# A delta-rule attention with two expert networks: a third expert's first 128 slots computed early, and another plan for all pieces

## The chip, the cores and the metric

One core of one Trainium2 chip. The metric is the device time of one execution in microseconds (us), the median of several runs. The core has five engines with an instruction stream each: PE (TensorE: matmuls, and weight loads that overlap them), DVE (VectorE), ACT (ScalarE), POOL (GpSimd) and SP (SyncE, which here only starts transfers). An engine executes its stream in order. If its next instruction has to wait, all that stands behind it in that stream waits too.

## The reference

```python
for t in range(768):                  # B=2, H=8, D=48
    y[:, :, t] = einsum(q_t, state)
    v_old = einsum(state, kn_t)
    state = state + beta_t * einsum(kn_t, v_t - v_old)
x = y -> (1536 tokens, 384)
h = x @ w_in                          # 384 -> 2048
P = a0 + a1*h + a2*h^2 + a3*h^3
Q = 1 + |b0|*|h| + |b1|*h^2
x = (P / (Q + 1e-6)) @ w_out          # 2048 -> 384
logits = x @ w_gate                   # 8 experts, argmax
disp[e, slot] = x of the tokens of e  # in token order, up to 384 slots
y = relu(disp @ w1[e]) @ w2[e]        # 384 -> 1024 -> 384
out[token] = prob * y[e, slot]
```

## The kernel before

The work is cut into pieces. Twelve chunks of 64 tokens make the attention; for each group of four chunks a triangular system is solved (`solve`, rounds 0, 1 and 2), with copies of the gram matrix on ACT (lines 247 and 249), turned on DVE (line 256), and results `A` that the next steps take. Two chunks of both batches make a block of 256 tokens, and there are six blocks (0 to 5).

The first network goes by tiles, eight for each block. `s1` computes `h` of a tile (18 matmuls of 256 columns, line 456); `e2` and `e3` compute the rational function with ACT (lines 461 to 483), DVE (465 to 476) and POOL (`zf` 463 and 464, `gl` 484), which leave the two halves `gh` and `gl`; `s2` multiplies them with `w_out` (`acct`, line 498, 12 matmuls a tile; in the last block `acc`, line 516, 18).

When a block is done, its gate runs: logits `lp` on PE (line 550), the choice `oh` on DVE (564), the place of each token among those of its expert (`pp` on PE, 617 to 620, then DVE and POOL), and a table of tokens by slot (`tb` on PE, 638), from which DVE writes the indices `idx` (645). POOL gathers the tokens of an expert by these indices with an indirect transfer. After the gate of block 3 `settle` already writes indices `idx0` (655), by which the first 128 slots of some experts are computed early: `early_x` gathers `ax` (749) and transposes it (`dxp`, 762), `early_h` is the first matrix (`ehp` on PE, 804, 72 matmuls of 128 columns in two halves, then ACT and DVE), `early_y` the second one (`y`, 821, 24 matmuls of 384 columns).

The experts' weights are loaded in eight pieces of 384 KB each (`ws`, line 739), and each is split by ACT (740) and DVE (741) into a high and a low half (`ew`). There is a ring of four staging buffers. All large memory is in six slots that are reused in turn: three of the attention, then that of the first matrix `wi`, then those of the second. The first two experts' weights go where two slots of the attention were, the early tokens (`ax`) into the third. When the last gate's `idx` is written, the rest follows: gathers `xd` (749), `dxp`, `hp` (784, 72 matmuls a group of slots), `hh` on ACT and `hl` on DVE (789, 790), `y`, and a scatter (827). An expert that has had its first 128 slots early has 128 left; the others have 256. The pieces of the other experts' weights are issued after `idx`, between these steps (`fill_`).

The order of all this comes from a table of times, `PLAN`. Each piece is entered with a time, the pieces that it needs, and a function that writes its instructions:

```python
def add(name, time, needs, f):
    todo[name] = (time, needs, f)
...
for name in sorted(todo, key=lambda q: todo[q][0]):
    emit(name)
```

A scheduler behind it then fixes the order on each engine. `EARLY` is the number of experts that begin early, `PLAN["experts"]` the number whose weights are pieces of the table.

Of the kernel before, what the change touches and what calls it, by code (L numbers as in the profile page):

```python
# [20 lines left out]
NCH = S // C  # L21
# [11 lines left out]
XS = 0.125  # L33

BYTOK = range(5)
PLAN = {'tiles': ((94.62, 6.95), (151.99, 6.94), (188.36, 5.73), (232.03, 5.29), (276.15, 3.92), (344.39, 2.58)),
 'lags': (8.77, 6.68, 15.4),
 'u': (50.59, 69.78, 81.54, 98.48, 107.98, 124.54, 157.18, 195.04, 218.05, 237.74, 249.51, 282.48),
 'rel': {'kT': 2.41,
         'loads': 4.55,  # L40
         'values': -10.66,
         'qk': -3.8,
         'lower': -5.93,
         'tk': -2.67,
         's': 10.18,
         'y': 3.45,
         'x': 7.22},
 'norm': (-36.92, 54.42, 110.21),
 'solve': ((-5.44, 3.69), (31.55, 6.74), (156.04, 3.59)),
 'gram': ((-1.03, 1.72), (14.91, 1.55), (123.21, 9.13)),  # L50
 'qk': (10.43, 32.45),
 'conv': (58.22, 0.02),
 'early': (8.43, 7.71),
 'lead': 16.47,
 'gate': (1.01, 2.5),
 'w': (364.51, 1.45),
 'experts': 2,
 'behind': 3,
 'masks': 2,
 'copies': 1,  # L60
 'settle': 310.33,
 'pre': ((362.66, 372.11, 354.38, 372.47), (338.34, 382.38, 397.83, 407.42)),
 'hold': 1}
WN = 4
CA = 2
HB = 3
ZB = 3
GB = 2
EARLY = 2
SETTLE = 3  # L70
ZA = 2
WS = 32.0
# [5 lines left out]
def attention_moe_moe(ctx, tc, kT, qT, k, v, beta, w_io, a, b, w_gate, w1, w2, out, dbg=None):  # L78
# [14 lines left out]
    def slot(shape, dt, name):  # L93
        return slots.tile(shape, dt, tag="slot", name=name)
# [40 lines left out]
    def load_kk(r):  # L135
        kk = st.tile([128, 2, 16, D], F32, tag="raw", name="kk", bufs=2)
        for i in range(2):
            kks[r, i] = kk[:, i]
            nc.sync.dma_start(kks[r, i], k[:, 4 * r + 2 * i:4 * r + 2 * i + 2].rearrange("p c u d -> p (c u) d"))
# [111 lines left out]
    def solve(r):  # L251

        gT = gams.pop(r)
        Wu = Wub[r % 2]
        nc.gpsimd.memset(bufB, 0.0)
        nc.vector.transpose(bufT, Wu.rearrange("p t u -> p (t u)"))
        Lt = bufT.rearrange("p (s t) -> p s t", s=32)
        A = bufA.rearrange("p (s t) -> p s t", s=32)
        nc.vector.scalar_tensor_tensor(A, Lt, -1.0, gT.unsqueeze(1).to_broadcast([128, 32, 32]), ALU.mult, ALU.mult)
        T = bufB.rearrange("p (t s) -> p t s", t=32)  # L260
        nc.vector.tensor_copy(bufB[:, 0:1024:33], gT)
        yield
        for j in range(31):
            m, n = 31 - j, j + 1
            tmp = bufT[:, 0:m * n].rearrange("p (i c) -> p i c", c=n)
            nc.vector.tensor_tensor(  # L266
                tmp, A[:, j, n:32].unsqueeze(2).to_broadcast([128, m, n]), T[:, j:n, 0:n].to_broadcast([128, m, n]), ALU.mult
            )
            nc.vector.tensor_tensor(T[:, n:32, 0:n], T[:, n:32, 0:n], tmp, ALU.add)  # L269
            if j % 4 == 3:  # L270
                yield
        nc.vector.transpose(Wu.rearrange("p t u -> p (t u)"), bufB)  # L272
        ends[r] = nc.vector.transpose(Tt, T.rearrange("p t s -> p s t"))
# [3 lines left out]
    def lower(n, tile_):  # L277
# [6 lines left out]
        for p in range(2):  # L284
            lo, hi = slice(64 * p, 64 * p + 32), slice(64 * p + 32, 64 * p + 64)
            for sl, o in ((lo, 0), (hi, 32)):
                if n < PLAN["copies"]:
                    nc.gpsimd.tensor_copy(Z[sl, :, p, o:o + 32], Wu[sl, :, us].rearrange("p t u -> p u t"))
# [46 lines left out]
    def qk(n, tile_):  # L335
# [6 lines left out]
        for p in range(2):  # L342
            o = slice(64 * p, 64 * p + 64)
            if n < PLAN["masks"]:
                nc.vector.tensor_tensor(G[o, :, p, :], g[o], mask[o].unsqueeze(1).to_broadcast([64, NP, C]), ALU.mult)
# [93 lines left out]
    TILES = []  # L439
# [213 lines left out]
    def settle(tile_):  # L653

        nc.vector.tensor_copy(idx0[:, 0:EARLY], tbl[:, 0:EARLY, 0])
        cn = tile_([128, EARLY], "cn0")
        nc.tensor.matmul(cn, ones16, osum[:, 0:EARLY], start=True, stop=True)
        ad = sm.tile([128, EARLY], F32, tag="mc", name="ad", bufs=1)
        nc.vector.tensor_scalar(ad, cn, -1.0, 128.0, ALU.mult, ALU.add)
        nc.vector.scalar_tensor_tensor(osum[0:1, 0:EARLY], ad[0:1], 0.0, osum[0:1, 0:EARLY], ALU.max, ALU.add)  # L660

# [82 lines left out]
    def gather(e, t0, nt, idx, to=None):  # L744
        res = []
        for t in range(nt):
            xd = to[t] if to else st.tile([128, ROW], F32, tag="t64", name="xd", bufs=3)
            col = idx.shape[-1] // E * e + t0 + t
            nc.gpsimd.indirect_dma_start(
                out=xd[:, :], out_offset=None, in_=rows[:, :], in_offset=bass.IndirectOffsetOnAxis(ap=idx[:, col:col + 1], axis=0),  # L750
            )
            res.append(xd)
        return res

    def expert_x(xds, ps, to=None):
        nt = len(xds)
        xh, xl = to or [el.tile([128, 3, SLOTS], F16, tag=f"x{i}", name="dx") for i in range(2)]
        gg = sm.tile([128, 2], F32, tag="gg", name="gg", bufs=3)
        for t, xd in enumerate(xds):
            xp = ps([128, DM], "dxp")  # L760
            for kt in range(3):
                nc.tensor.transpose(xp[:, 128 * kt:128 * kt + 128], xd[:, 128 * kt:128 * kt + 128], ident)
            cs = slice(128 * t, 128 * t + 128)
            src = xp.rearrange("p (k t) -> p k t", k=3)
            nc.scalar.activation(xh[:, :, cs], src, AF.Copy)
            nc.vector.tensor_tensor(xl[:, :, cs], src, xh[:, :, cs], ALU.subtract)
            nc.vector.tensor_copy(gg[:, t:t + 1], xd[:, DM:ROW])
        return xh, xl, gg
# [82 lines left out]
    def add(name, time, needs, f):  # L851
        todo[name] = (time, needs, f)
# [10 lines left out]
    first = {blk: next(i for i in range(len(TILES)) if TILES[i][0] == blk) for blk in range(len(BLOCKS))}  # L863
    tiles_at, lags = PLAN["tiles"], PLAN["lags"]
    T = [tiles_at[blk][0] + (i - first[blk]) * tiles_at[blk][1] for i, (blk, _) in enumerate(TILES)]
    U = PLAN["u"]
    r0 = PLAN["rel"]
    early = NCH and U[1] + r0["x"]
# [17 lines left out]
    add(("kk", 1), 2.0, [], lambda: load_kk(1))  # L886
    add(("kk", 2), PLAN["norm"][2] - 8, [("norm", 1)], lambda: load_kk(2))
    gens = {r: solve(r) for r in range(3)}
# [31 lines left out]
    for j in range(16):  # L920
        at = PLAN["early"][j] if j < len(PLAN["early"]) else c1 + dc * j
# [20 lines left out]
    def next_weights(e):  # L942
        if e not in wgen:
            wgen[e] = weights(e, got)
        next(wgen[e], None)

    for k_ in range(2 * WN * PLAN["experts"]):
        add(
            ("w", k_), PLAN["w"][0] + PLAN["w"][1] * k_ * 4 / WN, [("w", k_ - 1)] + [(c, n) for n in range(NCH) for c in ("y", "x")],
            lambda k_=k_: next_weights(k_ // (2 * WN))  # L950
        )

    ex, eh = {}, {}
# [3 lines left out]
    def early_x(e):  # L957
        if not ax:
            ax.append(slot([128, 6144], F32, "ax"))
        o = 1024 * EARLY + 1024 * e  # L960
        to = [ax[0][:, o + 512 + 192 * i:o + 704 + 192 * i].bitcast(F16).rearrange("p (k t) -> p k t", k=3) for i in range(2)]
        ex[e] = expert_x(gather(e, 0, 1, idx0, [ax[0][:, o:o + ROW]]), m_tile, to)

    def hold(e, f):
        if e < PLAN["hold"]:
            f()
        else:
            with tc.issue_after(ends["s2"].ins):
                f()

    def early_y(e):
        hh, hl = zip(*(eh[e, i] for i in range(2)))
        expert_y(e, 0, 1, (hh, hl), ex[e], got[e], idx0, lambda: None, m_tile)
# [5 lines left out]
    for e in range(EARLY):  # L979
        at = PLAN["pre"][e]  # L980
        wait = last_s2 if e >= PLAN["hold"] else []
        add(("ex", e), at[0], [("settle",), ("ex", e - 1)] + [("w", 2 * WN * (EARLY - 1))], lambda e=e: early_x(e))
        for i in range(2):
            add(("eh", e, i), at[1 + i], [("ex", e), ("eh", e, i - 1), ("ey", e - 2), ("w", 2 * WN * e + WN - 1)] + [("x", NCH - 1)] + wait,
                lambda e=e, i=i: hold(e, lambda: eh.update({(e, i): early_h(e, ex[e], got[e], i)})))
        add(("ey", e), at[3], [("eh", e, 1), ("w", 2 * WN * e + 2 * WN - 1)] + wait, lambda e=e: hold(e, lambda: early_y(e)))
# [32 lines left out]
    with tc.If(over > SLOTS):  # L1019
# [3 lines left out]
        for e in range(E):  # L1023
            run(weights(e, got2))
            for t0, nt in ((0, 2), (2, 1)):
                x = expert_x(gather(e, t0, nt, idx3), a_tile)
# [61 lines left out]
```

## Time and profile before

| | |
|---|---|
| median of 3 runs | 612.13 us (611.74 to 615.08) |
| the profiled execution | 612.29 us |
| its span, first to last instruction | 610.6 us |
| granted PE clock, mean | 0.909 of full |
| PE, DVE, ACT, POOL busy | 511.2, 464.3, 401.0, 289.7 us |
| moved by DMA | 59.33 MB |

The rows further down are from this one execution. A clock of 1.00 is 2.4 GHz and 0.50 is 1.2 GHz. Busy times overlap between engines. A row of a timeline may stand for several equal instructions in a row (x12), and its duration is then from the first one's start to the last one's end, with some 0.16 us of pipeline at the end of a matmul.

### The profile page before, as it was taken

What the parts mean: (1) busy time and instruction counts of PE and PEld (TensorE: products, weight loads), DVE (VectorE), ACT (ScalarE), POOL (GpSimd) and SP (SyncE); (2) the same over time, 40 slices, a digit from 0 to 9 for tenths busy, and PEclk for the clock granted to TensorE, in tenths of its full rate; (3) what the DMA queues carried; (4) which work ended last, traced back from release to release, by engine and by line L of the source; (5) the groups of instructions that cost most, each with busy time, mean ns of one, the idle gap of its engine ahead of it and who ended that gap; (6) DMA issues with size and microseconds to landing.
All of it is one profiled execution on the core that took longest, in us unless ns stands there. A gap on an engine that the chain in (4) does not pass through costs nothing.

```text
span 610.6 us, 14736 instructions
## 1 busy us (share of the span) xinstructions
PE 511.2 (84%) x5952; PEld 425.5 (70%) x5952; DVE 464.3 (76%) x868; ACT 401.0 (66%) x778; POOL 289.7 (47%) x282
## 2 busy tenths in 40 slices
PE   5415785888888998996999999989995998799993
PEld 5415674676667887885888888788884886567761
DVE  4899998999985999997657377999735777873320
ACT  6754667787889965858779779967641666661110
POOL 7402115877773765844546565668543222212111
PEclk9955557897989998999899999979998899999998
DMA  8911313555441010010020103370105788861001
GB/s 240 269 39 54 91 41 117 157 149 171 146 145 28 1 40 27 4 40 1 1 54 2 28 28 104 106 233 27 28 12 163 207 264 283 252 225 42 17 16 32
DMA packets 42159, 59.33 MB, mean 97 GB/s; under 512 B 25550, under 2 KB 29172, under 8 KB 42082
## 3 DMA queue, kind: packets, MB, share of 16 engines
q1 hardware_dynamic: 40034, 52.78, 28.9%
q0 software_dynamic: 2048, 5.52, 3.1%
q8 instruction: 49, 0.80, 0.6%
q14 instruction: 28, 0.23, 0.1%
HBM read 52.76 MB, written 6.30 MB: 97 GB/s over the span
## 4 chain that ended last, share of the span: by engine, by line
PE 37%; DVE 31%; DMA 12%; ACT 10%; issue 5%; POOL 2%; SPq 0%; POOLq 0%; DVEq 0%; ACTq 0%
PE h L456 8%; PE acct L498 7%; DMA ws<-in_w_dram 6%; PE y L821 6%; DVE A L266 6%; DVE A L269 5%; PE hp L784 4%; DMA raw<-in_w_io_dram 3%; ACT A L290 2%; DVE h L475 2%; DVE pf L465 2%; DVE ew L741 2%; PE acc L516 2%; DVE pf L474 2%; DVE pf L466 2%
## 5 line engine op out<-in xcount | busy, mean ns | idle before, releaser
L456 PE MATMUL h<-x,wi 128*128 128x256 f16 x864 | 117.1, 284 | 16.5 <-DVE wi L201 5.5
L456 PEld LDWEIGHTS <-wi 128*128 128x128 f16 x864 | 81.0, 101 | 36.8 <-issue 10.0
L484 POOL TENSOR_TENSOR gl<-pf,gh 128x512 fp32r<-128x512 f32 x48 | 65.5, 1365 | 47.5 <-ACT gh L483 42.0
L741 DVE SCALAR_TENSOR_TENSOR ew<-ws,ew 128x768 f16<-128x768 f32 x64 | 62.9, 997 | 17.3 <-ACT ew L740 16.9
L740 ACT ACTIVATE ew<-ws 128x768 f16<-128x768 f32 x64 | 52.9, 841 | 23.3 <-DMA ws<-in_w_dram 22.7
L784 PE MATMUL hp<-dx,ew 128*128 128x256 f16 (+1 forms) x576 | 59.8, 265 | 9.1 <-DVE hl L790 8.3
L463 POOL TENSOR_SCALAR zf<-za,cf 128x512 f32<-128x512 f32 x48 | 42.1, 876 | 52.6 <-ACT za L461 52.2
L464 POOL TENSOR_TENSOR zf<-zf,za 128x512 f32<-128x512 f32 x48 | 65.0, 1353 | 3.7
L784 PEld LDWEIGHTS <-ew 128*128 128x128 f16 x576 | 52.5, 101 | 16.1 <-issue 10.1
L827 POOL DMA_INDIRECT out_dram<-yo,idx x16 | 18.5, 1158 | 84.5 <-DVE yo L825 70.2
L821 PE MATMUL y<-ew,hh 128*128 128x384 f16 x224 | 55.9, 326 | 0.0
L474 DVE SCALAR_TENSOR_TENSOR pf<-pf,cf,h 128x512 f32<-128x512 f32 x48 | 35.5, 739 | 17.2 <-ACT h L473 16.9
L465 DVE TENSOR_TENSOR pf<-pf,h 128x512 f32<-128x512 f32 x48 | 32.4, 676 | 16.1 <-ACT pf L462 12.8
L498 PE MATMUL acct<-wo_h,gh 128*128 128x384 f32 x160 | 42.2, 379 | 1.7 <-ACT gh L483 1.6
L266 DVE TENSOR_TENSOR A<-A,A 128x31 f32<-128x31 f32 (+15 forms) x93 | 41.2, 443 | 2.3
L269 DVE TENSOR_TENSOR A<-A,A 128x31 f32<-128x31 f32 (+15 forms) x93 | 41.0, 440 | 2.4
L472 ACT ACTIVATE za<-zf,qc 128x512 f32<-128x512 f32 x48 | 34.6, 721 | 11.7 <-POOL zf L464 11.4
L498 PE MATMUL acct<-wo_h,gl 128*128 128x384 f32 x160 | 39.1, 356 | 2.1 <-POOL gl L484 2.1
L323 POOL TENSOR_TENSOR A<-v,nrm 64x384 f32<-64x384 f32 x24 | 23.2, 967 | 35.8 <-PE S L373 26.3
L290 ACT ACTIVATE A<-A 32x256 f32<-32x256 f32 x44 | 28.7, 651 | 16.3 <-DVE A L272 13.1
L789 ACT ACTIVATE hh<-hp 128x512 f16<-128x512 f32 (+1 forms) x32 | 16.9, 536 | 32.9 <-PE hp L784 32.9
L462 ACT ACTIVATE pf<-h,cf 128x512 f32<-128x512 f32 x48 | 37.2, 775 | 1.0 <-POOL gl L484 0.9
(188 smaller groups left out, 1271.3 us busy)
## 6 DMA issues: line engine op xcount, KB each, us to landing
ws<-in_w_dram SPq DMA_DIRECT2D x64, 384.0 KB, 4.1
raw<-in_w_io_dram SPq DMA_DIRECT2D x16, 768.0 KB, 4.6
rows<-xr SPq DMA_DIRECT2D x12, 192.5 KB, 2.9
kk<-in_k_dram SPq DMA_DIRECT2D x6, 384.0 KB, 4.6
A<-in_k_dram SPq DMA_DIRECT2D x24, 96.0 KB, 2.8
v<-in_v_dram SPq DMA_DIRECT2D x12, 192.0 KB, 3.2
A<-in_qT_dram SPq DMA_DIRECT2D x24, 96.0 KB, 2.8
A<-in_kT_dram SPq DMA_DIRECT2D x10, 192.0 KB, 3.6
```

What stands on the lines that cost most here:

```text
L266: nc.vector.tensor_tensor(tmp, A[:, j, n:32].unsqueeze(2).to_broadcast([128, m, n]), T[:, j:n, 0:n].to_broadcast([128, m, n]), ALU.mult)
L269: nc.vector.tensor_tensor(T[:, n:32, 0:n], T[:, n:32, 0:n], tmp, ALU.add)
L456: s1_last[i] = nc.tensor.matmul(h[:, w * m:w * m + w], ww[:, kt, js], x[:, kt, 0:w], start=(n == 0), stop=(n == 8))
L464: nc.gpsimd.tensor_tensor(zf, zf, za, ALU.mult)
L465: nc.vector.tensor_tensor(pf, pf, h, ALU.mult)
L474: nc.vector.scalar_tensor_tensor(pf, pf, cf[:, 0:1], h, ALU.add, ALU.mult)
L484: nc.gpsimd.tensor_tensor(gl, pf, gh.bitcast(F32), ALU.subtract)
L498: ends["s2"] = nc.tensor.matmul(acc[blk][t], g[:, o:o + 128], ww[:, j, :], start=(j == 0 and m == 0), stop=(j == 15 and m == 2))
L740: nc.scalar.activation(ws[:, 2 * m, cs], s, AF.Copy, scale=MS)
L741: nc.vector.scalar_tensor_tensor(ws[:, 2 * m + 1, cs], s, MS, ws[:, 2 * m, cs], ALU.mult, ALU.subtract)
L784: nc.tensor.matmul(hp[:, g, 0:ns], w[:, kt, 128 * (f + g):128 * (f + g) + 128], xx[:, kt, 0:ns], start=(n == 0), stop=(n == 8))
L821: nc.tensor.matmul(y, hx[f // 4][:, f % 4, cs], w[:, f, :], start=(n == 0), stop=(n == 23))
```

## The change

Three experts instead of two have their first 128 slots computed early, and the weights of the third go as pieces of the table into the slot of `wi`. That slot is free when the last `s1` has been done, so its eight pieces wait for that and for the first early gather. All numbers of the plan are new. The diff without the larger part of the plan's numbers:

```diff
-PLAN = {'tiles': ((94.62, 6.95), (151.99, 6.94), ...
+PLAN = {'tiles': ((87.39, 6.96), (135.34, 7.24), ...
...
- 'experts': 2,
+ 'experts': 3,
+ 'w2': (378.99, -0.47),
  'behind': 3,
  'masks': 2,
- 'copies': 1,
- 'settle': 310.33,
- 'pre': ((362.66, 372.11, 354.38, 372.47), (338.34, 382.38, 397.83, 407.42)),
- 'hold': 1}
+ 'copies': 3,
+ 'settle': 272.89,
+ 'pre': ((322.1, 322.01, 316.46, 336.37), (277.99, 342.7, 356.3, 363.26), (333.47, 349.5, 364.59, 405.2)),
+ 'hold': 4}
...
-EARLY = 2
+EARLY = 3
+
+FIRST = 2
...
     for k_ in range(2 * WN * PLAN["experts"]):
         add(
-            ("w", k_), PLAN["w"][0] + PLAN["w"][1] * k_ * 4 / WN, [("w", k_ - 1)] + [(c, n) for n in range(NCH) for c in ("y", "x")],
+            ("w", k_), PLAN["w"][0] + PLAN["w"][1] * k_ * 4 / WN if k_ < 2 * WN * FIRST else PLAN["w2"][0] + PLAN["w2"][1] * (k_ - 2 * WN * FIRST),
+            [("w", k_ - 1)] + [(c, n) for n in range(NCH) for c in ("y", "x")] + [("s1", len(TILES) - 1), ("ex", 0)] * (k_ >= 2 * WN * FIRST),
             lambda k_=k_: next_weights(k_ // (2 * WN))
         )
...
-        add(("ex", e), at[0], [("settle",), ("ex", e - 1)] + [("w", 2 * WN * (EARLY - 1))], lambda e=e: early_x(e))
+        add(("ex", e), at[0], [("settle",), ("ex", e - 1)] + [("w", 2 * WN * (FIRST - 1))], lambda e=e: early_x(e))
```

What moves is seen in the order of the instructions. In the changed kernel the lines have numbers that are higher by 3 (by 4 after line 949).

On PE, at the end, between the last gate's place matmuls (`pp`, line 618) and the first `dxp` of gathered rows, the order before is this; of each run of equal matmuls the first is shown (12 `ehp`, 12 `y`, `tb`, 12 `y`):

```order
L618 MATMUL pp<-oh,low_136 128x16
L620 MATMUL pp<-oh,ones_138 128x8
...
L804 MATMUL ehp<-ax,ew 128x128
...
L821 MATMUL y<-ew,ax 128x384
...
L638 MATMUL tb<-v_5759,pm 128x8
...
L821 MATMUL y<-ew,ax 128x384
...
L762 MATMUL dxp<-ident,xd 128x128 x3
```

In the changed kernel the same place reads as follows (6 `ehp`, 12 `y`, 11 `ehp`, `y`, `ehp`, `tb`, 11 `y`, 24 `ehp`, 13 `y`, and 11 `y` behind the first three `dxp`):

```order
L621 MATMUL pp<-oh,low_136 128x16
...
L807 MATMUL ehp<-ax,ew 128x128
...
L641 MATMUL tb<-v_5765,pm 128x8
...
L824 MATMUL y<-ew,ax 128x384
...
L807 MATMUL ehp<-ax,ew 128x128
...
L824 MATMUL y<-ew,ax 128x384
...
L765 MATMUL dxp<-ident,xd 128x128 x3
...
L824 MATMUL y<-ew,ax 128x384
```

Between the last `acc` and `tb` there were 72 `ehp` and 12 `y`; now there are 120 and 13. Behind `tb` there are 24 `ehp` that were not there.

On PE, in the gate of block 3, between the logits `lp` and the place matmul `pp` that takes `oh`, there were 18 `h` and 12 `acct` matmuls, and steps of the last chunk (`Y`, `xp`):

```order
L550 MATMUL lp<-wg,xT 128x8 x6
...
L456 MATMUL h<-x_3589,wi 128x256
...
L498 MATMUL acct<-wo_h,gh 128x384 x4
...
L400 MATMUL xp<-ident,ys 128x128
L403 MATMUL xp<-ident,ys 64x64 x2
...
L618 MATMUL pp<-oh,low_136 128x16
```

Now 46 `h` of later tiles and 26 `acct` stand there:

```order
L553 MATMUL lp<-wg,xT 128x8 x3
...
L459 MATMUL h<-x_3631,wi 128x256
...
L501 MATMUL acct<-wo_h,gh 128x384 x4
...
L459 MATMUL h<-x_4442,wi 128x256
...
L501 MATMUL acct<-wo_h,gl 128x384 x4
...
L459 MATMUL h<-x_4441,wi 128x256
...
L621 MATMUL pp<-oh,low_136 128x16
```

More of the first network's work has moved in between, and the chunk's steps have moved out.

On ACT, in solve round 2, the copies of the gram (lines 247 and 249) stood in a row behind an `h` (line 473); the rows show that `h`, the first of six such rows of three copies, and what follows the fourth:

```order
L473 ACTIVATE h<-za 128x512
L247 ACTIVATE A_87<-gram 32x8x32 x2
L249 ACTIVATE A_87<-gram 32x256
...
L483 ACTIVATE gh<-pf 128x512
L472 ACTIVATE za<-zf,qc 128x512
```

Now two of these rows of three stand ahead of the `h` of the same tile (line 476 of the changed kernel):

```order
L250 ACTIVATE A_87<-gram 32x8x32 x2
L252 ACTIVATE A_87<-gram 32x256
...
L464 ACTIVATE za<-h 128x512
L465 ACTIVATE pf<-h,cf 128x512
L476 ACTIVATE h<-za 128x512
L410 ACTIVATE x_1878<-xp 128x3x64
```

Six copies have moved ahead of it, and twelve are left behind it.

## Rows read from the trace of the kernel before

**Rows 1.** The page's first part: engine, busy us, share of the span, instructions.

```profile
PE 511.2 (84%) x5952; PEld 425.5 (70%) x5952; DVE 464.3 (76%) x868; ACT 401.0 (66%) x778; POOL 289.7 (47%) x282
```

**Rows 2.** Windows; stretch, length, busy us of PE, PEld, DVE, ACT, POOL, PEclk, DMA.

```profile
200.00:283.00 83.00, 78.79 (x855) 67.73 (x852) 82.35 (x163) 58.71 (x116) 54.18 (x52) 0.98 0.09 21
...
473.00:550.00 77.00, 67.76 (x589) 54.16 (x590) 60.52 (x94) 49.58 (x77) 18.05 (x16) 0.96 0.79 245
```

**Rows 3.** PE's waits (whole span, then 270 to 460): us, times, longest.

```profile
PE hp L784 <- DVE hl L790: 8.3, 3, 4.0
...
PE e L300 <- ACT A L304: 3.6, 1, 3.6
PE pp L618 <- DVE oh L564: 2.7, 1, 2.7
...
PE dxp L762 <- DMA ax<-rows,idx: 0.9, 2, 0.8
```

**Rows 4.** Windows behind three waits of PE; columns as in rows 2.

```profile
288.10:294.90 6.80, 6.80 (x81) 5.46 (x77) 3.26 (x5) 4.85 (x9) 4.53 (x5) 0.50 0.00 0
...
398.50:404.10 5.60, 5.60 (x19) 5.60 (x19) 5.60 (x12) 3.17 (x6) 4.45 (x5) 0.50 0.62 181
...
473.00:479.20 6.20, 5.50 (x42) 4.94 (x43) 3.94 (x9) 3.56 (x6) 1.94 (x2) 0.50 0.57 188
```

**Rows 5.** PE's timeline at the end: start, us, line, operation, [idle before <-releaser].

```profile
437.92 4.13 PE L804 MATMUL ehp<-ax,ew 128*128 128x128 f16 x71
...
453.77 0.38 PE L516 MATMUL acc<-gl,wo_h 128*128 128x256 f32 x1 [0.85 <-POOL gl L484]
...
455.66 0.28 PE L516 MATMUL acc<-gh,wo_l 128*128 128x256 f32 x1
...
463.93 0.24 PE L638 MATMUL tb<-v,pm 128*128 128x8 f16 x4
464.03 2.11 PE L821 MATMUL y<-ew,ax 128*128 128x384 f16 x12
472.99 0.87 PE L762 MATMUL dxp<-ident,xd 128*128 128x128 f32 x3 [6.85 <-DMA xd<-rows,idx]
...
560.40 8.02 PE L784 MATMUL hp<-dx,ew 128*128 128x256 f16 x72
```

**Rows 6.** PE's timeline: two of three `hp` that waited for `hl`.

```profile
511.57 2.13 PE L784 MATMUL hp<-dx,ew 128*128 128x256 f16 x18 [2.70 <-DVE hl L790]
...
532.42 2.12 PE L784 MATMUL hp<-dx,ew 128*128 128x256 f16 x18 [4.01 <-DVE hl L790]
```

**Rows 7.** DVE's timeline: `idx`, and the weight pieces 24 and 33 to 34.

```profile
464.21 0.17 DVE L645 TENSOR_TENSOR idx<-tbl,tb 128x16 uint32<-128x16 f32 x1 [0.40 <-PE tb L638]
...
508.90 0.96 DVE L741 SCALAR_TENSOR_TENSOR ew<-ws,ew 128x768 f16<-128x768 f32 x1 [0.91 <-ACT ew L740]
...
523.18 1.94 DVE L741 SCALAR_TENSOR_TENSOR ew<-ws,ew 128x768 f16<-128x768 f32 x2
```

**Rows 8.** ACT's and DVE's timeline in solve round 2.

```profile
186.87 1.24 ACT L247 ACTIVATE A<-gram 32x256 f32<-32x256 f32 x2
...
188.58 0.74 DVE L466 SCALAR_TENSOR_TENSOR pf<-pf,cf,h 128x512 f32<-128x512 f32 x1
...
196.65 1.25 DVE L256 STREAM_TRANSPOSE A<-A 128x1024 f32<-128x1024 f32 x1 [6.73 <-ACT A L247]
```

**Rows 9.** Timelines of PE, DVE and POOL: indices and gathers, early and last.

```profile
409.09 0.24 PE L638 MATMUL tb<-v,pm 128*128 128x8 f16 x4
...
410.73 0.15 DVE L655 CAST idx<-tbl 128x2 uint32<-128x2 f32 x1
...
429.08 1.17 POOL L749 DMA_INDIRECT ax<-rows,idx  x1 [1.88 <-issue]
...
433.74 0.52 PE L762 MATMUL dxp<-ident,ax 128*128 128x128 f32 x3 [0.76 <-DMA ax<-rows,idx]
...
465.68 1.32 POOL L749 DMA_INDIRECT xd<-rows,idx  x1 [4.86 <-DVE ew L741]
```

More of the change, by code (lines that the diff above doesn't have):

```diff
@@ L35 @@
 BYTOK = range(5)
[L36 to L39, printed above, removed]
+PLAN = {'tiles': ((87.39, 6.96), (135.34, 7.24), (173.58, 5.61), (228.86, 5.43), (261.99, 3.31), (304.16, 2.45)),
+ 'lags': (7.85, 6.14, 15.25),
+ 'u': (50.56, 68.24, 74.12, 91.1, 101.22, 117.16, 149.8, 190.86, 211.68, 233.44, 248.05, 258.63),
+ 'rel': {'kT': 1.1,
          'loads': 4.55,
-         'values': -10.66,
+         'values': -10.08,
          'qk': -3.8,
-         'lower': -5.93,
+         'lower': -6.09,
          'tk': -2.67,
-         's': 10.18,
+         's': 4.15,
          'y': 3.45,
[L47 to L56, printed above, removed]
- 'experts': 2,
+         'x': 9.91},
+ 'norm': (-25.56, 44.75, 94.01),
+ 'solve': ((-22.39, 0.64), (42.7, 7.45), (165.7, 2.86)),
+ 'gram': ((-14.02, 7.74), (23.31, 1.73), (115.83, 7.46)),
+ 'qk': (5.57, 34.64),
+ 'conv': (31.48, 1.38),
+ 'early': (5.78, 5.58),
+ 'lead': 13.0,
+ 'gate': (0.7, 3.03),
+ 'w': (291.4, 7.94),
+ 'experts': 3,
+ 'w2': (378.99, -0.47),
  'behind': 3,
  'masks': 2,
- 'copies': 1,
- 'settle': 310.33,
- 'pre': ((362.66, 372.11, 354.38, 372.47), (338.34, 382.38, 397.83, 407.42)),
- 'hold': 1}
+ 'copies': 3,
+ 'settle': 272.89,
+ 'pre': ((322.1, 322.01, 316.46, 336.37), (277.99, 342.7, 356.3, 363.26), (333.47, 349.5, 364.59, 405.2)),
+ 'hold': 4}
 WN = 4
```

## The prediction

> **What bounds the kernel now.** The page's table of engines came first: TensorE (PE) is busy 511.2 of 610.6 us [rows 1], so what can be won is PE's idle time, PE's work at the low clock, and work that PE need not do. The busy time by stage came next. Between 200 and 283 us PE is busy 78.79 of 83 us and VectorE (DVE) 82.35: DVE is full there, and PE goes at its pace. From 473 to 550 us (the experts behind the last gate) PE is busy 67.76 of 77 and DVE 60.52 [rows 2]. The lists of waits tell which idle time has a cause the change touches: 8.3 us in three waits of an expert's `hp` for `hl`, and between 270 and 460 us 3.6 us for `A` (solve round 2), 2.7 us for `oh` (gate of block 3) and 0.9 us for the early gathers [rows 3]. The windows behind such gaps show a second price. After the waits of 3.6, 2.7 and 6.85 us the granted clock reads 0.50, the 1.2 GHz level instead of 2.4, for 6 to 7 us with PE nearly all the time busy [rows 4]: 5.6 us of work there would be 2.8 at the full clock, so such a spell costs about 3 us beside the wait. The wait of 0.85 us for `gl` [rows 5] was followed by none.
>
> The chain at the end, in PE's timeline [rows 5]: the last `acc` matmul of the first expert network starts at 455.66, `tb` of the last gate at 463.93, DVE writes `idx` at 464.21 [rows 7], and the first `dxp` of gathered rows starts at 472.99, after a gap of 6.85 us. From there on PE works and waits to its end near 600.3, 136.1 us behind `idx`, and the kernel ends with it. What stands ahead of `tb` delays everything behind it; what stands between `tb` and `dxp` is free as far as the gap reaches; what stands behind is paid in full.
>
> **The end, term by term**, against the profiled 612.29 us (0.16 over the median).
>
> (1) Ahead of `tb`, PE now has 120 `ehp` matmuls instead of 72 behind the last `acc`, and 13 `y` instead of 12. 71 `ehp` took 4.13 us, 0.16 of it the end of the pipeline: 0.056 us each. 12 `y` took 2.11 and in the same way 1.95, 0.1625 each [rows 5]. 48 x 0.056 + 0.16 = **+2.85**.
>
> (2) Between `tb` and `dxp` stand 24 `ehp` and 24 `y` instead of 12 `y`: 5.24 us instead of 1.95. The gathers leave as long after `idx` as before, so the gap shrinks from 6.85 to about 3.6 and the end doesn't move: **0**. I keep the low clock behind it, since 2.7 and 3.6 were followed by it; without it about -3.
>
> (3) Behind the gather, the third expert has one tile of 128 slots left instead of two. A full expert's 72 `hp` of 256 columns take 8.02 us with the pipeline's end, 7.86 without [rows 5]; a 128-column expert takes 72 x 0.056 = 4.03. `hp`: 6 x 7.86 + 2 x 4.03 = 55.2 before, 5 x 7.86 + 3 x 4.03 = 51.4 after. `y`: 14 tiles of 24, 3.9 us each, against 13, of which 11 matmuls moved behind the first `dxp` (1.8): 54.6 and 52.5. `dxp`: one tile of three transposes less, 0.33. In all **-6.3**.
>
> (4) The `hl` waits: 2.70, 4.01 and 1.64 us (the first two in [rows 6]). `hl` stands on DVE behind weight pieces. Before, it came behind 25, 38 and 48 pieces in experts 3, 4 and 5. The changed kernel has 40 pieces in place of 48 left, since the third expert's eight land earlier, and has 24 and 33 ahead of `hl` of experts 3 and 4. The pieces come at the pace of their transfers: the 24th ended 45.6 us behind `idx`, the 33rd 59.9 behind (the first of a pair in its row) [rows 7], and an `hl` takes 0.6 more. At expert 3, PE stood there 44.7 us behind `idx` (511.57 - 2.70 - 464.21); the third expert's shorter `hp` (7.86 - 4.03), the transposes and (5) take 4.7 off and the 11 `y` and some waiting of its narrow groups put up to 2.9 on: 42.9, a wait of 3.3 us to 46.2. At expert 4 it stands some 12.5 us later (18 `hp` 2.0, transposes 0.7, one tile of `y` 3.9, 54 `hp` 5.9): 58.7 against 60.5, 1.8 us. At expert 5 nothing is left to wait for. 5.1 for 8.35, **-3.25**. Bounds: all 8.35 gone, or a wait as long as before.
>
> (5) The 11 `y` behind the first `dxp` cover the wait for `dx` there, 0.58 us: **-0.6**.
>
> The end: **-7.3** (+2.85 - 6.3 - 3.25 - 0.6). Bounds -12 (no low clock, less waiting for pieces) and 0 (the waits for `hl` grow by what (3) saves).
>
> **Ahead of the end.** (6) Solve round 2. ACT (ScalarE) makes 18 copies of the gram from 186.87 on, nearly in a row, and DVE idles 6.73 us for them until 196.65 [rows 8]. The `h` (natural exponential) ahead of all 18 has 6 of them ahead of it in the changed order and 12 behind, 3.3 us less after the tile work that DVE waits with, so that about half of the wait goes. Seven tile operations of DVE, 0.66 us each (0.74 with the part that overlaps the next [rows 8]), that stood between the start and the end of the solve stand behind it: 4.6 us. But PE comes to the step that needs the solve's result after 1.2 tiles of `h` and one of `acct` less, 22 x 0.11 + 12 x 0.16 = 4.3 us by the 256 and 384 columns of [rows 5], so the earlier result first makes up for a shorter cover. I take **-3** (0 when the cover is what binds, -9 when the 3.6 us wait of [rows 3] goes with its spell too and the rest).
>
> (7) Gate of block 3. PE waits 2.7 us for `oh` [rows 3] and then runs at the low clock [rows 4]. Behind `lp` stood 18 `h` and 12 `acct`, now 46 and 26: by the 0.11 us of 256 columns and the 0.1625 of 384 [rows 5] 3.9 and 9.3 us, less some 2 of the chunk's steps that have gone, so that 3.4 us more cover 2.7. 2.7 + 2.8 would be 5.5; **-4**, because DVE is full there and `oh` itself may come later. Bounds -6 and 0.
>
> (8) The early gathers. `tb` of gate 3 started at 409.09 and `idx0` at 410.73, done some 1.8 us later than the former, from `idx` to the gather 1.5 us (464.21 to 465.68 at the last gate), and from the gather's start to the second `dxp` 4.7 us (429.08 to 433.74) [rows 7, 9]. That is 8 us; before, 20 us of other work lay between `tb` and the gather. In the changed order PE has from that `tb` to the first `dxp` 18 `h`, 4 `acct`, 19 `acc` and a few small ones, 5.2 us at these prices. **+3** less 0.8 of the wait that it replaces, so **+2.2**; +5.2 when the low clock follows.
>
> (9) The last tile's `gl`: 72 `ehp` of expert 0 (4 us) now stand between the `acc` groups and could cover the wait of 0.85 [rows 5], but weight pieces now stand on ACT and DVE in front of this tile's `gh`. I leave the wait as it is and count the third expert's `dxp`: **+0.4**.
>
> Sum ahead of the end: -3 - 4 + 2.2 + 0.4 = **-4.4**. Altogether -11.7: **600.6 us**.
>
> **One price that could be wrong.** The split of an expert's pass of 256 columns into two of 128 rests on 0.056 us for a 128-column matmul with its weight load [rows 5]. The Trainium skill, "TensorE: Matmul & The Clock Gate", section "Back-to-back issue gap", gives about 81 ns for a stream of weight load and matmul at 128 columns, and says that 56 ns holds for an isolated one alone. By it 144 matmuls would cost an estimated 11.7 us in place of 8.1. This trace disagrees: 71 in a row took 0.056 us each. Were the price of a 128-column stream 0.025 us higher, term (1) would be +1.2, and terms (2) and (3) by 48 more matmuls some 1.8 worse: 603.6 us.
>
> **Rivals.**
> A. *The tail alone pays*: terms (6) to (9) cancel, because DVE is full up to 283 us [rows 2] and what PE saves at one place it waits for at the next. 612.29 - 7.3 = 605.0.
> B. *The last tile is late*. The third expert's pieces now stand on DVE ahead of the last tile's last polynomial step (two of them) and on ACT ahead of its `gh` (two more). If these land at the pace of the tail's pieces, 1.9 us (45.6 us over 24, [rows 7]), `gl` comes 4.3 us later, 3.5 of it beyond the cover, with a spell of 3 behind: 600.6 + 6.5 = 607.1, near the edge of no change.
> C. *Slower*: between 200 and 283 us. DVE is full there, and the changed order puts the steps of ten tiles 3.5 to 7 us of DVE work later. PE, with 4.2 us idle [rows 2], would run dry: 7 us of waits and three spells of 3 give +16, 616.6. It ends slower by over 0.5% from 14.8 us of new idle time and spells on; for it speaks that every gap near 3 us there has its spell, against it that DVE's total at the milestones of each block stays within a few us.
> D. *The change doesn't do what it says*: the third expert's weights, which wait for the last `h` matmul and the first early gather, aren't there for the 72 `ehp` ahead of `tb`. Eight pieces at 1.9 us each are 15 us; between the last `h` and that place lie 18 to 20 us of PE's work [rows 5]. A miss of 5 us there would give 605.6.
> E. *By the price above*: 603.6.
>
> **How the numbers follow.** The forecast as summed has 0.48, A 0.20, B 0.10, C 0.12, D 0.05, E 0.03, better than 595 us 0.02. The forecast's own range is 595 to 606 (terms (4), (6) and (7) between their bounds). A change of 0.5%, 3.06 us, is about what the three runs (611.74 to 615.08) can tell from none: faster is below 609.23 and slower above 615.35. Faster: 0.48 + 0.20 + half of B + D, E and the better case, 0.83, of which I take 0.07 off for terms that I may have missed: 0.76. Slower: C nearly whole, 0.11. Same: 0.13. The range leaves out C and the far end: 592 to 612.
>
> **What would show it.** (1) `tb` of the last gate some 2.85 us later behind the last `acc`. (2) A gap of about 3.6 us before `dxp`, clock 0.50 behind it. (3) and (4): PE's end some 126 us behind `idx` in place of 136, and two waits for `hl`. (6) The wait of DVE for the gram copies halved. (7) No wait for `oh` and no 0.50 near 400 us. (8) A wait of 2 to 3 us for `ax`. Wrong would be: PE less than 78 us busy in the 83 us up to 283 (C), a wait of `acc` for `gl` of over 2 us (B), or a wait of `ehp` for `ew` (D).

## The result, and the profile after

The changed kernel takes 606.75 us (median of 4 runs, 604.26 to 607.29) against 613.36 for the kernel before (4 runs beside it, 611.74 to 615.08): a ratio of 0.9884, 95% interval 0.9841 to 0.9927. It is 1.2% faster. Ratios, here and below, are of fast executions alone and so need not be the quotient of two medians, which are of all of them. The profiled execution took 604.26 us (the shortest of its four), 8.03 less than the one of before, and that difference splits at one place, the last `acc` matmul.

The changed kernel's timeline of PE (start, us, line, operation, idle before it and its releaser) answers to [rows 5]:

```profile
444.97 4.18 PE L807 MATMUL ehp<-ax,ew 128*128 128x128 f16 x72
...
452.75 4.06 PE L824 MATMUL y<-ew,ax 128*128 128x384 f16 x24 [0.96 <-DVE ax L812]
...
458.68 0.28 PE L519 MATMUL acc<-gh,wo_l 128*128 128x256 f32 x1
...
469.79 0.24 PE L641 MATMUL tb<-v,pm 128*128 128x8 f16 x4
...
471.68 1.50 PE L807 MATMUL ehp<-ax,ew 128*128 128x128 f16 x24
...
476.81 0.52 PE L765 MATMUL dxp<-ident,xd 128*128 128x128 f32 x3 [1.52 <-DMA xd<-rows,idx]
```

The last `acc` starts at 458.68 where it was 455.66, 3.02 us later. PE's last matmul (PE's end, below) starts at 592.21 where it was 600.18, so the stretch behind `acc` is 10.99 us shorter.

Within that stretch: `acc` to `tb` is 11.11 us where it was 8.27 (+2.84). `idx` to the first `dxp` is 6.74 where it was 8.78 (-2.04). From there to PE's end it is 115.40 where it was 127.19 (-11.79). DVE's and POOL's timelines of the changed kernel, and SP's, show why the second is shorter; they answer to [rows 7, 9]:

```profile
470.07 0.17 DVE L648 TENSOR_TENSOR idx<-tbl,tb 128x16 uint32<-128x16 f32 x1 [1.51 <-PE tb L641]
470.71 1.28 POOL L752 DMA_INDIRECT xd<-rows,idx  x1 [4.18 <-DVE idx L648]
471.14 2.94 SPq L742 DMA_DIRECT2D ws<-in_w_dram  x4
```

The first gather now starts 0.64 us behind `idx`, ahead of the four weight pieces. Before, it started 1.47 behind `idx` [rows 9].

The waits for `hl`, in PE's timeline (they answer to [rows 6], 8.35 us before):

```profile
501.99 1.17 PE L787 MATMUL hp<-dx,ew 128*128 128x128 f16 x18 [0.96 <-DVE hl L793]
...
506.64 4.09 PE L787 MATMUL hp<-dx,ew 128*128 128x256 f16 x36 [0.71 <-DVE hl L793]
...
525.70 2.12 PE L787 MATMUL hp<-dx,ew 128*128 128x256 f16 x18 [2.86 <-DVE hl L793]
```

They sum to 4.53 us. The windows of the changed kernel (columns as in [rows 2]):

```profile
200.00:283.00 83.00, 75.77 (x836) 65.46 (x836) 82.21 (x157) 55.91 (x112) 51.12 (x49) 0.98 0.09 20
...
456.00:473.00 17.00, 17.00 (x217) 15.12 (x215) 10.67 (x33) 6.69 (x13) 3.90 (x7) 1.00 0.32 101
473.00:550.00 77.00, 69.22 (x647) 54.24 (x645) 56.07 (x92) 43.97 (x72) 21.17 (x20) 1.00 0.71 231
```

Two things are to be seen: the clock behind the last gap is 1.00 (the spell at 0.50 of [rows 4] is gone in this execution), and PE is 3 us less busy between 200 and 283 us than before, while DVE is as full.

At the gate of block 3, `pp` has no wait any more, but two others stand in front of it, and the clock is at half behind them (PE's timeline, and a window):

```profile
386.82 1.01 PE L388 MATMUL Y<-A,A 112*64 112x48 f32 x16 [1.22 <-ACT A L365]
388.84 0.47 PE L403 MATMUL xp<-ident,ys 128*128 128x128 f32 x1 [1.00 <-ACT ys L390]
...
409.88 0.17 PE L621 MATMUL pp<-oh,low 128*128 128x16 f16 x1
```

```profile
388.80:395.00 6.20, 6.16 (x33) 4.58 (x34) 6.20 (x8) 6.03 (x11) 3.40 (x3) 0.53 0.40 121
```

### The profile page after: what moved, and what is told of

It is laid out like the page before. It is cut to its first block, busy times and chain, and to the rows that moved or that the text cites. A ratio compares the mean times of both kernels' runs of the same rounds, so it can differ in the third digit from the quotient of the medians.

```text
span 602.5 us, 14884 instructions
## 1 busy us (share of the span) xinstructions
PE 503.4 (84%) x6024; PEld 421.3 (70%) x6024; DVE 472.2 (78%) x870; ACT 393.4 (65%) x772; POOL 293.0 (49%) x290
## 4 chain that ended last, share of the span: by engine, by line
DVE 38%; PE 30%; ACT 12%; issue 8%; DMA 7%; POOL 4%; SPq 0%; DVEq 0%; POOLq 0%; ACTq 0%
PE y L824 7%; DVE A L272 7%; DVE A L269 7%; PE h L459 6%; DMA ws<-in_w_dram 4%; PE hp L787 4%; DVE ew L744 4%; PE acct L501 4%; ACT A L250 3%; DVE h L478 2%; DVE pf L468 2%; DVE pf L469 2%; DVE pf L479 2%; DVE pf L477 2%; POOL zf L467 1%
## 5 line engine op out<-in xcount | busy, mean ns | idle before, releaser
L459 PE MATMUL h<-x,wi 128*128 128x256 f16 x864 | 115.0, 284 | 9.0 <-ACT x L410 3.8
L744 DVE SCALAR_TENSOR_TENSOR ew<-ws,ew 128x768 f16<-128x768 f32 x64 | 68.4, 1089 | 11.5 <-ACT ew L743 11.2
L466 POOL TENSOR_SCALAR zf<-za,cf 128x512 f32<-128x512 f32 x48 | 44.2, 922 | 65.0 <-ACT za L464 64.3
L787 PE MATMUL hp<-dx,ew 128*128 128x256 f16 (+1 forms) x576 | 53.8, 252 | 6.1 <-DVE hl L793 4.5
L787 PEld LDWEIGHTS <-ew 128*128 128x128 f16 x576 | 47.8, 98 | 11.6 <-issue 6.9
L824 PE MATMUL y<-ew,hh 128*128 128x384 f16 x208 | 51.7, 326 | 0.0
L272 DVE TENSOR_TENSOR A<-A,A 128x31 f32<-128x31 f32 (+15 forms) x93 | 44.6, 479 | 2.4
L269 DVE TENSOR_TENSOR A<-A,A 128x31 f32<-128x31 f32 (+15 forms) x93 | 44.2, 476 | 2.5
L501 PE MATMUL acct<-wo_h,gh 128*128 128x384 f32 x160 | 40.8, 370 | 1.7 <-ACT gh L486 1.7
L501 PE MATMUL acct<-wo_l,gh 128*128 128x384 f32 x160 | 38.6, 356 | 0.0
L476 ACT ACTIVATE h<-za 128x512 f32<-128x512 f32 x48 | 28.6, 596 | 12.0 <-DVE pf L469 8.4
```

Source lines behind the costliest of these rows:

```text
L269: nc.vector.tensor_tensor(tmp, A[:, j, n:32].unsqueeze(2).to_broadcast([128, m, n]), T[:, j:n, 0:n].to_broadcast([128, m, n]), ALU.mult)
L459: s1_last[i] = nc.tensor.matmul(h[:, w * m:w * m + w], ww[:, kt, js], x[:, kt, 0:w], start=(n == 0), stop=(n == 8))
L501: ends["s2"] = nc.tensor.matmul(acc[blk][t], g[:, o:o + 128], ww[:, j, :], start=(j == 0 and m == 0), stop=(j == 15 and m == 2))
L744: nc.vector.scalar_tensor_tensor(ws[:, 2 * m + 1, cs], s, MS, ws[:, 2 * m, cs], ALU.mult, ALU.subtract)
L787: nc.tensor.matmul(hp[:, g, 0:ns], w[:, kt, 128 * (f + g):128 * (f + g) + 128], xx[:, kt, 0:ns], start=(n == 0), stop=(n == 8))
L824: nc.tensor.matmul(y, hx[f // 4][:, f % 4, cs], w[:, f, :], start=(n == 0), stop=(n == 23))
```

## Experiments

Eight kernels. Ratios are against the kernel before on the same chip, with their 95% intervals.

**Each half of the change alone.** The new plan with two early experts:

```diff
- 'experts': 3,
+ 'experts': 2,
...
-EARLY = 3
+EARLY = 2
```

> The new plan with two early experts, as before. Theory: the new plan by itself puts the last acc about 3 us later and pays nothing at the end, 614 to 617 us. Rival: the new plan carries the gain by itself, 605 to 609 us.

Measured: 615.16 us, ratio 0.9991 (0.9959 to 1.0023). Its last `acc` starts at 456.57, 0.91 us later than before and not 3; `idx` to PE's end is 136.21 us (135.97 before). So the theory had the time right, and the plan alone neither pays nor costs more than the 2.5 us that the interval leaves open.

The old plan with a third early expert:

```diff
- 'experts': 2,
+ 'experts': 3,
+ 'w2': (420.0, -0.47),
...
- 'pre': ((362.66, 372.11, 354.38, 372.47), (338.34, 382.38, 397.83, 407.42)),
+ 'pre': ((362.66, 372.11, 354.38, 372.47), (338.34, 382.38, 397.83, 407.42), (374.5, 390.5, 405.6, 446.2)),
...
-EARLY = 2
+EARLY = 3
...
```

> The old plan with a third early expert added (its pieces and steps at the new plan's distance behind the last tile). Theory: the third expert alone takes 11 us off the end (2.8 later at tb, 13.8 less from idx to the end) and nothing is lost ahead of it: 601 to 604 us. Rival: it gains only with the new plan, because here its pieces or its steps come too late: 609 to 614 us.

Measured: 614.45 us, ratio 0.9986 (0.9949 to 1.0023). The theory had the end right in sign and not in size, and was wrong about what lies ahead; the rival's claim, that it gains only with the new plan, held. `acc` to `tb` is 11.49 and `idx` to PE's end 125.79, so that in all the stretch behind the last `acc` is 6.96 us shorter. But that `acc` starts at 466.77, 11.11 us later than before. ACT's and PE's timeline of this run show where part of it went:

```profile
459.06 0.84 ACT L743 ACTIVATE ew<-ws 128x768 f16<-128x768 f32 x1 [1.51 <-DMA ws<-in_w_dram]
459.81 0.47 ACT L768 ACTIVATE ax<-dxp 128x384 f16<-128x384 f32 x1
460.23 0.84 ACT L743 ACTIVATE ew<-ws 128x768 f16<-128x768 f32 x1
460.98 0.61 ACT L486 ACTIVATE gh<-pf 128x512 fp32r<-128x512 f32 x1
...
461.65 0.50 PE L519 MATMUL acc<-gh,wo_h 128*128 128x256 f32 x2 [3.20 <-ACT gh L486]
...
463.40 0.58 PE L519 MATMUL acc<-gl,wo_h 128*128 128x256 f32 x1 [1.25 <-POOL gl L487]
```

The last tile's `gh` stands on ACT behind pieces of the third expert that wait for their transfers, and PE waits 4.45 us for it and for `gl`. This is rival B, in the old plan. In the changed kernel `gh` comes behind such pieces too, but PE has the 72 `ehp` and 24 `y` of expert 0 to do meanwhile. Of the 11.11 us, 3.01 were there before the order differs on DVE, ACT or POOL (the same `pp` at 401.50 where it was 398.49, last section). Of the other 8.10, 3.60 are these waits (0.85 before); the rest was not taken apart, but the granted clock is 0.83 from 433 to 443 us and 0.60 from 461.2 to 467.

Put together, the four kernels say more than each half. In the new plan too the third expert can be seen by itself, because the plan alone and the changed kernel have the same order on DVE, ACT and POOL up to 443 us. Counted from the `pp` of block 3's gate (407.62 and 409.88) the last `acc` starts 48.95 us later with two early experts and 48.80 with three: nothing is lost. In the old plan it is 57.17 and 65.27. From `idx` to PE's end the third expert takes 14.07 us off in the new plan and 10.18 in the old one. So what the plan is worth is that it takes up the third expert's work ahead of the end, where the old plan pays 8.10 us for it.

**The cover.** The old plan with three experts again, with expert 0's early matmuls moved behind the last tile's `h`:

```diff
- 'pre': ((362.66, 372.11, 354.38, 372.47), ...
+ 'pre': ((362.66, 373.5, 376.0, 378.0), ...
```

> The old plan with a third early expert (the run that gained nothing), with expert 0's 72 early matmuls moved from ahead of the last tile's h to between its acc groups, as in the changed kernel. Theory: the third expert's pieces hold up gh of the last tile by some 5 us on ACT and DVE, and the changed kernel pays nothing for it only because PE has these 72 matmuls to do meanwhile; with the cover the acc waits of 3.2 and 1.25 us and the low clock behind them go, 606 to 610 us. Rival: what the old plan with three experts loses is lost earlier: 612 to 615 us.

Measured: 611.32 us, ratio 0.9955 (0.9926 to 0.9983). The waits of `acc` for the last tile are down to 0.67 us, as the theory had it, but the time lies between theory and rival: a wait of 2.28 us of `y` for `ax` comes in its place, and the clock in the windows from 430 to 450 us is 0.81 and 0.85 behind the waits for the early gathers. From the common `pp` (399.79) to the last `acc` it is 64.92 us, against 65.27 in the run before it, so in the profile the cover won almost nothing; the ratio is lower than that run's 0.9986, but the two intervals overlap. The reverse, the changed kernel with those matmuls moved ahead of the last tiles' `h`:

```diff
- 'pre': ((322.1, 322.01, 316.46, 336.37), ...
+ 'pre': ((322.1, 300, 300, 336.37), ...
```

> The changed kernel with expert 0's 72 early matmuls moved ahead of the last tiles' h, so that they no longer stand between the last tile's acc groups. Theory: PE then waits 3 to 5 us for gh and gl of the last tile, with a spell of low clock behind: 610 to 614 us. Rival: the cover isn't needed, 605 to 608 us.

Measured: 614.86 us, ratio 0.9986 (0.9947 to 1.0024), a little over the theory's range, so the whole gain is gone. PE's, DVE's and POOL's timelines, and a window of it:

```profile
451.34 0.27 PE L641 MATMUL tb<-v,pm 128*128 128x8 f16 x4 [3.20 <-DVE pm L634]
...
447.87 3.42 DVE L634 TENSOR_TENSOR pm<-ps,io 128x512 f16<-128x512 f32 x1
...
448.24 2.49 POOL L487 TENSOR_TENSOR gl<-pf,gh 128x512 fp32r<-128x512 f32 x2
...
463.88 1.04 POOL L830 DMA_INDIRECT out_dram<-yo,idx  x1 [13.16 <-DVE yo L828]
464.93 1.29 POOL L487 TENSOR_TENSOR gl<-pf,gh 128x512 fp32r<-128x512 f32 x1
...
466.27 0.38 PE L519 MATMUL acc<-gl,wo_h 128*128 128x256 f32 x1 [3.09 <-POOL gl L487]
```

```profile
450.00:460.00 10.00, 8.66 (x44) 5.67 (x45) 9.77 (x14) 3.51 (x5) 0.72 (x1) 0.66 0.64 188
```

The wait for `gl` has the expected size but another cause. ACT's `gh` ends at 460.83, and POOL begins `gl` only at 464.93, because the scatter of expert 0's rows stands ahead of it and waits for `yo`. The wait of `tb` for `pm`, with the low clock behind it, was not expected. The 72 matmuls had not covered it: in the changed kernel they stand behind this `tb` (444.86, then `ehp` from 444.97). There `pm` took 0.68 us on DVE and here 3.42, with two `gl` on POOL at the same time. The last `acc` starts at 468.58, 9.9 us later than in the changed kernel, while `idx` to PE's end is 122.65 us, as there (122.14). So the place of these matmuls is worth the whole gain, but this run does not show that they are worth it as a cover for `gh`: by moving them it changed what waits for what on POOL and DVE too.

**What stands ahead of `tb`.** The kernel before with work added there and nothing else:

```diff
+        if last:
+            dm = a_tile([128, DM], "dm")
+            for i in range(18):
+                nc.tensor.matmul(dm, pm[:, 0, 0:128], got[0][2][:, 0, :], start=(i == 0), stop=(i == 17))
         tb = tile_([128, 2, E], "tb")
```

> The kernel before with 18 matmuls of 384 columns added ahead of the last tb, into a tile that nothing reads (2.9 us of PE work, as much as the change adds there; nothing of the result changes). Prediction's step: all of it delays the end, idx to the first dxp stays at 8.8 us and idx to the end at 136. Theory: in the kernel before it is not idx that releases the last gather but the transfer of the block's rows, which lands 1 us behind idx, by when four weight pieces stand ahead of the gather; with tb 2.9 us later the gather starts 0.4 to 0.6 us behind idx and ahead of them, idx to dxp is 6 to 7 us, and the end comes about 1 us later instead of 2.9.

Measured: 615.14 us, ratio 1.0022 (0.9991 to 1.0054). `acc` to `tb` is 11.20 us, 2.93 more, and from the end of `acc` to PE's end 143.86 where it was 144.24: in the profile nothing of the 2.93 arrives. (2.63 come back at the gather, below, and 0.68 behind `dxp`. The medians, 615.14 and 614.54, differ by 0.6; the interval reaches up to 3.3 us, so the times alone decide nothing here.) PE's and POOL's timeline, and a window:

```profile
468.55 0.24 PE L642 MATMUL tb<-v,pm 128*128 128x8 f16 x4
469.27 1.48 POOL L753 DMA_INDIRECT xd<-rows,idx  x1 [6.75 <-DVE idx L649]
...
474.98 0.90 PE L766 MATMUL dxp<-ident,xd 128*128 128x128 f32 x3 [4.22 <-DMA xd<-rows,idx]
```

```profile
474.00:480.00 6.00, 3.62 (x24) 3.05 (x25) 2.38 (x6) 2.44 (x4) 2.96 (x3) 0.50 0.93 312
```

`idx` (468.83) to `dxp` is 6.15 us where it was 8.78: the gather starts 0.44 us behind `idx`. In the kernel before it started 1.47 behind. The second transfer of the last block's rows, which the gather reads, was issued there about 462.9 and such a one took 2.3, so it landed about 465.2; the gather followed at 465.68, and the four weight pieces had started at 465.27. The same split runs through all ten kernels: in four (this one, the changed kernel, no cover, and the changed kernel with copies 1) the gather starts 0.44 to 0.64 us behind `idx`, and `idx` to `dxp` is 5.92 to 6.74 us; in the six others it starts 1.14 to 2.04 behind, and `idx` to `dxp` is 8.22 to 8.99. In those six the profile names an `ew` step of DVE as the releaser, but the first of these starts 0.08 or 0.09 us behind `idx` in all ten, and the weight pieces start 1.06 or 1.07 behind it in all ten. What differs is the rows' transfer: in the four SP has issued it 2.4 to 4.2 us ahead of `idx`, in the six only 1.3 to 2.0, and there the gather starts 2.7 to 3.3 us behind that issue. The gap of 4.22 us still has the low clock behind it.

**The low clock behind the gap.** The kernel before with 40 matmuls added between `tb` and `dxp`:

```diff
+    with tc.issue_after(ends["idx"].ins):
+        dm = a_tile([128, DM], "dm")
+        for i in range(40):
+            nc.tensor.matmul(dm, got[0][2][:, 0, 0:128], got[0][2][:, 0, :], start=(i == 0), stop=(i == 39))
```

> The kernel before with 40 matmuls of 384 columns added between the last tb and the first dxp of gathered rows, into a tile that nothing reads (6.5 us of PE work in the gap of 6.85; nothing of the result changes). Theory: the gap costs a second time by the low clock behind it, so that with PE busy the granted clock stays at 1.00 behind dxp and the time is about 3 us shorter, 611 against 614, idx to the end 133 us for 136. Rival: the clock falls all the same or nothing behind dxp gains by it, because hl and the weight pieces set the pace there: no change or 1 to 2 us more.

Measured: 618.42 us, ratio 1.0025 (0.9988 to 1.0062). This doesn't decide whether the spell costs anything: the scheduler put nine transposes `dxp` in a row behind the added work in place of three and then `hp`, and PE's timeline has new waits there, with the low clock behind them:

```profile
476.38 1.02 PE L762 MATMUL dxp<-ident,xd 128*128 128x128 f32 x6 [1.74 <-DMA xd<-rows,idx]
...
480.55 5.60 PE L784 MATMUL hp<-dx,ew 128*128 128x128 f16 x51 [2.97 <-DVE dx L766]
```

The gap itself was closed (0.24 us), and the gathers behind the first set the pace instead.

**The copies on POOL.** One number of the new plan taken back, and the same number put into the old plan:

```diff
- 'copies': 3,
+ 'copies': 1,
```

> The changed kernel with one of three POOL copies per solve round taken back (copies 1 as before, all else of the new plan). Theory: the copies on POOL slow DVE's solve steps that run at the same time (lines 269 and 272 of the changed kernel took 88.8 us in the first 283 us where before they took 82.0) and DVE is full there, so the last acc comes 3 to 4 us earlier and the time is 602 to 604 us. Rival: the order of tiles and chunks in the new plan costs it, not the copies: 605 to 608 us, solve steps slower or not.

```diff
- 'copies': 1,
+ 'copies': 3,
```

> The kernel before with copies 3 and nothing else. Theory: the solve steps take 5 to 7 us more of DVE and the time is 615 to 617 us. Rival: the copies cost nothing, since ACT is relieved as much as DVE is slowed: 611 to 614 us.

Measured: 617.12 us (ratio 1.0034, 1.0007 to 1.0061) and 626.61 us (1.0190, 1.0140 to 1.0239). The first is 10 us slower than the changed kernel and the second 10 us over its theory; neither theory nor rival held in either. DVE's 186 solve steps take 82.0 us before, 88.8 in the changed kernel, 81.3 with copies back at 1; but put into the old plan copies 3 makes 83.5 of 82.0. The theory's cause is wrong for most of this. The number counts chunks: with 3, chunks 0 to 2 have their four copies each on POOL, between 51 and 68 us in the changed kernel, and no later chunk has any. Of the 6.8 us that the changed kernel's steps take more, 4.8 lie in solve round 2 (200 to 281 us), where POOL makes no copies and runs `zf` and `gl`. The times say nothing of the copies either: each number re-deals thousands of rows of the order on PE, and the run with copies 1 waits 4.47 us for the last tile's `gl`. Neither run measures the copies by themselves.

## Why the prediction came out as it did

The sign and the range held (600.6 forecast, 606.75 measured, 592 to 612). The two halves of the sum did not: the end gave -10.99 for -7.3, and what lies ahead of it +3.02 for -4.4. That their sum came within 6 us is in part luck, since one half missed by 3.7 and the other by 7.4 the other way.

The step that failed is "Sum ahead of the end: -3 - 4 + 2.2 + 0.4 = -4.4". The plan alone moves the last `acc` by +0.9 us and the time not at all, and 2.26 of the 3.02 were there at the same `pp` of two equal orders (409.88 and 407.62), so they are no work of the third expert. Rival A (terms (6) to (9) cancel) is the nearest, at 605.0 for 606.75 measured, but it kept the end at -7.3, so its number is in part luck too. Waits alone, (6) to (9) gave -1.3, -0.5, +0.8 and +0.1. Term by term:

- (6) DVE's wait for the gram copies fell from 6.73 to 2.6 us, somewhat more than forecast, and PE's wait of 3.6 became one of 2.3 at about the same place, with a shorter spell behind it (granted clock 0.74 over the next 6.5 us). That the earlier copies for the most part made up for the shorter cover is read from these rows and was not tested.
- (7) The wait for `oh` went, as forecast; two waits of 1.22 and 1.00 us some 20 us earlier took its place, with a clock of 0.53 behind them. I had priced the removed wait with its spell, as if the spell belonged to the wait. It does not: behind these two waits the clock was 1.00 in the plan alone, and behind the wait for `oh` it was 1.00 in two of five kernels (last section). My own trace had waits of 2.70 and 4.01 us [rows 6] with 1.00 behind them.
- (8) The waits for the early gathers are 0.81 us for `ax` and 0.94 for `gg`, 1.75 for 0.9 before: +0.8, not +2.2.
- (9) The wait of `acc` for `gl` went, and one of `y` for `ax` (0.96) came.

The sign that I had set for C was there (PE 75.77 us busy between 200 and 283, under 78), but it is no sign of C: the plan alone shows 73.47 there and is no slower. In the changed kernel PE's longest waits in that stretch are 1.9 us for `oh`, 1.7 in two for `gh` and 1.2 for `A`.

At the end, most mechanisms were right and sizes off:

- (1) The added work ahead of `tb` took 2.84 us for 2.85 forecast, but "what stands ahead of `tb` delays everything behind it" is wrong: 2.04 came back, because the rows' transfer and not `idx` had released the gather. The run with added work shows it by itself, in its profile.
- (2) The gap became 1.52 us and not 3.6, by the earlier gather, and the clock stayed at 1.00. I had kept the spell. By estimate it cost 2.7 us before (5.50 us of work at 0.50, [rows 4]); the run that was to test this did not decide.
- (3) and (4) From `dxp` to the end 11.79 us went. My 6.3 for the shorter expert, 3.82 for the `hl` waits (3.25 forecast) and 2.7 for the clock make 12.8; a wait for `dx` of 1.46 us in place of 0.58 takes 0.9 back (term (5) had it vanish). Of these terms only the waits are measured.
- D did not come: the third expert's `ehp` show no wait for `ew`. B came in the old plan, as waits of 4.45 us behind a late `gh`. In the changed kernel weight pieces stand ahead of `gh` too and PE does not wait; that the 72 `ehp` and 24 `y` cover it is read from the order, and no run shows it by itself.
- The price of a 128-column stream held: 72 in 4.18 us here, 0.056 each. By the Trainium skill, "TensorE: Matmul & The Clock Gate", section "Back-to-back issue gap", it would be an estimated 5.8 us; the measurement decides. (Rival E's 1.8 us in terms (2) and (3) are 72 matmuls at 0.025, not 48; its 603.6 stands.)

So neither half pays alone. The third expert takes work off the end but lays eight weight pieces on ACT and DVE in front of the last tile. The plan's worth is that this costs nothing ahead of the end, which the four kernels show; which of its numbers does it is open.

## What to carry to other kernels

Before work ahead of a transfer's issue is counted as delay, find which of its inputs is last: here an index was charged with what another transfer held up, and 2.9 us of added work did not reach the end of the profile. Do not price a wait with the low-clock spell behind it in one profile: the same wait can stand without one in the next. When a change lays loads on engines that still finish an earlier stage, look for the matmuls that can stand in that place, and test each half and the pair: here only the four kernels together show what the plan is worth.

## What the runs showed of the hardware that was not expected

The length of a gap in PE's work does not settle the clock behind it. The wait of `pp` for `oh` at the gate of block 3 is 2.72 to 2.74 us in five kernels with the same order there. Behind it the granted clock was 0.50, 0.50 and 0.53 (1.2 GHz nearly throughout) in the kernel before, the third expert alone and the cover, and 1.00 in the two with added work, which comes only later. In the kernel before it was 1.00 behind the wait of 4.01 us for `hl`, too (windows of the run with 40 added matmuls, of the one with 18, and of the kernel before; columns as in [rows 2]):

```profile
398.90:404.90 6.00, 5.29 (x28) 4.31 (x28) 6.00 (x12) 3.48 (x6) 4.45 (x5) 1.00 0.64 190
...
399.40:405.40 6.00, 5.25 (x28) 4.27 (x28) 6.00 (x11) 3.53 (x6) 4.47 (x5) 1.00 0.66 193
...
532.40:538.40 6.00, 5.98 (x44) 4.23 (x44) 4.75 (x7) 3.28 (x5) 1.64 (x2) 1.00 0.87 290
```

The gap before `dxp` was followed by 0.50 where it was 4.22 to 6.85 us long and by 1.00 where it was 1.52.

DVE's solve steps take two to three times as long while POOL works beside them. DVE's timeline of the changed kernel (line 272) beside POOL's copies:

```profile
65.42 2.66 POOL L291 COPY A<-A 32x256 f32<-32x256 f32 x4 [3.15 <-PE U L364]
65.53 0.60 DVE L272 TENSOR_TENSOR A<-A,A 128x60 f32<-128x60 f32 x1
66.17 0.67 DVE L269 TENSOR_TENSOR A<-A,A 128x87 f32<-128x87 f32 x1
```

In the kernel before, with POOL idle there, the same steps took 0.22 and 0.25 us. Each now takes about as long as one copy (2.66 / 4 = 0.67). Counted over the 186 steps of the changed kernel's timeline, the 131 that run beside no POOL instruction stay within 0.04 us of the shortest of their size; the 55 others are 25.8 us longer in all, 10.0 of it beside `gl` and 8.3 beside `zf`. In the kernel before it is 19.5 us. The `pm` of 3.42 us above is another case. The Trainium skill, "SBUF — State Buffer", section "SBUF: two separate sides", says that a DVE instruction with two inputs from that memory and a GpSimd one that reads it hold a shared port in turn, each for its whole instruction; the trace agrees.

Executions of one order drift apart. Up to the gate of block 3 five of these kernels have the same order on DVE, ACT and POOL, and the same `pp` starts there at 398.49, 398.93, 399.38, 399.79 and 401.50 us. Three kernels share the new plan's order as far (the changed kernel, the plan alone, no cover), and there it starts at 409.88, 407.62 and 408.64. A difference of 3 us in one profile's stage is therefore no finding by itself, and the +3.0 and +0.9 of the last `acc` are to be read with that.
